# Attention and MLP decode: narrow matrix-vector products widened to 28 copies, the folded MLP weight rows loaded at the start, one scalar step moved

## The chip, the cores and the metric

The kernel runs on one core of one Trainium2 chip. The metric is the device time of one execution in microseconds (us), as the median of several runs; lower is better.

## The reference

One decode step for 8 requests. An attention block and an MLP block alternate, and both are applied twice with the same weights and the same caches:

```python
x = x + A(layernorm(x));  x = x + B(layernorm(x))     # layer 0
x = x + A(layernorm(x));  x = x + B(layernorm(x))     # layer 1
# A: q = x @ wq (448 -> 16 heads of 256); scores against k_cache (8 heads, 4096 keys, 256 wide,
#    two query heads on each), softmax, times v_cache, @ wo (4096 -> 448)
# B: hs = shifted(gelu(layernorm(x) @ w1)) @ w2;  x1 = x + hs
#    x1 + gelu(layernorm(x1) @ w3) @ w4              (448 -> 1792 -> 448)
```

With one token per request the shifts bring in zeros alone, so the kernel computes no w1 and no w2. One request's K cache is 16 MB in bf16, its V cache as much. Each layer needs all of both, for all 8 requests.

## The kernel before, in words

**Tiles and slots.** The unit of loading is a quarter of one head's K or V: 128 partitions of 2048 bf16 values, 512 KB. On-chip memory has 30 slots of that size (`QUARTERS`). The queue of SyncE (SP) loads the units in a fixed order into free slots (`load`, `issue_kv`, line 645); up to four units of one head become one load if neighbouring slots are free at that moment (`next_kv`). Some K and V units of a request (`KEEP_K`, `KEEP_V`) stay in their slots from layer 0 to layer 1, so that they are read once. A slot is freed by the PE instruction that reads it last, and SP waits for that instruction before it loads the slot again.

**One head.** `front` transposes K on TensorE (PE, L1509), VectorE (DVE) and ScalarE (ACT) copy the result back into the slot (L1440, L1441), PE makes the scores (in rows, L1405, or in 48 columns, L1148), and DVE, GpSimd (POOL) and ACT make the softmax. `back` multiplies by V (PV, L1275: eight matmuls with 256 columns per unit, four of them side by side in the array), adds the four partial rows (L1311) and multiplies by wo (L1339).

**Requests.** For each request b the kernel does layer 0 of some heads, then `mid(b)`, which is the layer 0 MLP and the layer 1 queries, and then layer 1, mixed with layer 0 of the next request. While `mid(b)` runs, the V units of the next request's heads arrive one by one as loads of 512 KB, each into a slot that a PV has just freed.

**The narrow products.** In `mid` a single vector of 448 or 1792 values meets a weight matrix. The weights are the stationary operand (128x128 blocks), the vector is the moving operand, one column wide. The kernel lets the same column stream several times (`bcast`, a step of zero), which gives as many equal result columns. Three families use it: the queries (`q_mms`, L901, `QW` copies, from `second_queries` and `column_sums`), the first MLP product (`h_mms`, L917, `HW` copies, called H here) and the second MLP product (`y_mm` in `mlp`, L1065, `YW` copies, called Y). Q and H step by one column from block to block: the copies of a block are overwritten by the next block, and only the first column of each stays. Y steps by `YW` columns, so its five blocks lie side by side. The last MLP, for two requests together, uses `HW // 2` columns (`dst is None`), the one for six requests uses none.

**Folded rows.** 448 = 3 x 128 + 64. The last 64 rows of w3 lie folded in `w3x_sb`: columns 0 to 895 on partitions 0 to 63, columns 896 to 1791 on partitions 64 to 127. wq's last rows lie in `wqx_sb` in the same way; there one half is loaded by SP and the other by ACT's queue, both at the start (`load_wq`). w3x is loaded by SP, both halves, with w3 (`load_rest`, due place 18).

**The order of the work.** `Plan` records every operation with a priority and a duration in microseconds, and `schedule` writes down the order of each engine in advance. `pe()` gives a narrow product n matmuls times `width` columns; the planner adds the columns of each piece of 3.413 us and takes the full-clock duration if the piece before had at least 3000 (`COLS`). Where PE is idle for over 0.1 us it puts in fillers (L1716, identity matmuls without use for the result) unless the last 3.413 us already hold 3500 columns (`TARGET`). The slots, and so how many units one load takes, follow from the planned times.

**The end.** After the last head, `last_stats`, `mlp(dst=None)`, `last_scale(1)` and `last_rows` make the last two requests' output: tanh on ACT (L1037), hT on DVE (L1046), four scalars `lin` on DVE (L828, L830, L836) that scale the residual row `xs` (L965), 56 matmuls (L973) and the sum `o_last` (L979).

Of the kernel before, what the change touches and what calls it, by code (L numbers as in the profile page):

```python
# [6 lines left out]
P = 128  # L7
B = 8
D = 448
# [3 lines left out]
NC5 = 5  # L13
# [32 lines left out]
LAST_AT = (-3, -2, -1)  # L46
PV0 = 0
PV1 = 0
QW, HW, YW = 24, 24, 12
SC = 448  # L50
YC = 0
ST = 504
# [423 lines left out]
def bass_interleave_layers__gqa_block_cached__mixer_s_mlp__decode_kernel(  # L476
# [20 lines left out]
    plan = Plan()  # L497
# [6 lines left out]
    def sb(name, shape, dt):  # L504
        n = 4 if dt in (f32, i32) else 2
        for s in shape[1:]:
            n *= s
        al = 32 if n >= 128 else 8
        cursor[0] = (cursor[0] + al - 1) // al * al
        t = nc.alloc_sbuf_tensor_at(name, shape, dt, offset=cursor[0], align_bytes=al)  # L510
        cursor[0] += (n + al - 1) // al * al
        assert cursor[0] <= high0, (name, cursor[0], high0)
        return t
# [5 lines left out]
    w3x_sb = sb("w3x_sb", [P, F // 2], bf)  # L519
    w4_sb = sb("w4_sb", [P, 14 * D], bf)  # L520
# [30 lines left out]
    lin = sb("lin", [P, 2, 2], f32)  # L551
# [5 lines left out]
    hT = sb("hT", [P, NB], bf)  # L557
# [54 lines left out]
    def bcast(ap, shape, axis):  # L612

        dims = [list(x) for x in ap.ap]
        dims.insert(axis, [0, shape])
        return bass.AP(tensor=ap.tensor, offset=ap.offset, ap=dims)
# [8 lines left out]
    def dma(name, dst, src, nbytes, sem, val, wr, at, row=8192):  # L625

        us = nbytes / 16 / 26.88e3 + nbytes / row / 16 * 0.008
        plan.op("sp", lambda eng: eng.dma_start(dst, src), us / FASTER, name, wr=wr, prio=at,  # L628
                dma=(sem, val))

    def dma_once(name, parts, keys, at, also=()):

        for i, (dst, src, nbytes, *row) in enumerate(parts):
            dma(name, dst, src, nbytes, nc.alloc_semaphore(f"s_{name}{i}"), 16,
                [keys[i], *(also if i == 0 else ())], 4 * at - 0.5, *row)
# [49 lines left out]
    def const_c(v):  # L685
# [7 lines left out]
            wr=["sel"])  # L693
# [7 lines left out]
    for bank, key in [(psR, "R"), (psM, M)]:  # L701
        plan.op("dve", lambda v, bank=bank: v.memset(bank[:, :], 0.0), 0.5, "const",
                wr=["psM", ("row", 0), ("row", 1)], banks=[key])
# [7 lines left out]
    def dv(fn, dur=0.13, rd=(), wr=(), banks=(), name="chain", prio=None):  # L711
        if prio is None:
            prio = urge[0] + len(plan.ops)
        return plan.op("dve", fn, dur, name, rd=rd, wr=wr, banks=banks, prio=prio)
# [6 lines left out]
    def pe(fn, n, rd=(), wr=(), banks=(), name="chain", prio=None, width=20):  # L721

        if prio is None:
            prio = urge[0] + len(plan.ops)
        d = 0.06 + 0.026 * n
        return plan.op("pe", fn, (d, max(d, 0.06 + n * width / 1200), width * n, n), name, rd=rd, wr=wr, banks=banks, prio=prio)
# [59 lines left out]
    def factor(k, c, v, rd, dv=dv):  # L786


        x, t, y = (z[:, k, c:c + 1] for z in (var, rst, rsy))
        a, b = (KK * (1.0 + LN_EPS) / D, KK * LN_EPS * LN_EPS) if k else (KK / D, KK * LN_EPS)  # L790
        dv(lambda e: e.tensor_scalar(x, v, a, b, ALU.mult, ALU.add), rd=rd, wr=[("x", k, c)])
        newton(x, t, y, ("t", k, c), [("x", k, c)], ("y", k, c), dv)
# [26 lines left out]
    def last_scale(r):  # L819


        c = B - 2 + r
        y, sf = rsy[:, 0, c:c + 1], self_f[:, r:r + 1]
        mm = mom[:, 2, 4 * r + 1:4 * r + 2]
        if r == 0:
            factor(0, c, mom[:, 2, 4 * r:4 * r + 1], [("v", r)])
        add = self_f[:, 0:1] if r == 0 else lin[:, 0, 0:1]
        dv(lambda v: v.tensor_scalar(lin[:, r, 0:1], y, sf, add, ALU.mult, ALU.add),  # L828
           rd=[("y", 0, c), "sel_f"] + [("lin", 0, 0), "hT"] * r, wr=[("lin", r, 0)])
        dv(lambda v: v.tensor_scalar(lin[:, r, 1:2], y, sf, mm, ALU.mult, ALU.mult),  # L830
           rd=[("y", 0, c), ("mm", r), "sel_f"], wr=[("lin", r, 1)])
        if r == 0:
            dv(lambda v: v.tensor_tensor(lin[:, 0, 0:1], lin[:, 0, 0:1], self_f[:, 1:2], ALU.add),
               rd=[("lin", 0, 0), "sel_f"], wr=[("lin", 0, 0)])
        else:
            dv(lambda v: v.tensor_tensor(lin[:, 1, 1:2], lin[:, 1, 1:2], lin[:, 0, 1:2], ALU.add),  # L836
               rd=[("lin", 0, 1), ("lin", 1, 1)], wr=[("lin", 1, 1)])
# [148 lines left out]
    def mlp(src, skey, n, dst, dkeys, rows_open=False):  # L986

        few = n < 3
        ch, kb, bk = where[0]
        at = SC if few else 0  # L990
        yw, yc = (YW, SC) if few else (n, 0)
        m = 14 * n
        h_, a_, hT_ = (hb[:, 0:m], g1[:, 0:m], hT) if few else (hb6[:, 0:m], g16[:, 0:m], hT6)
        GK, HK = (["g1", "xc", "yb"], ["hT"]) if few else (KH, KH)
# [4 lines left out]
        if dst is None:  # L999
# [3 lines left out]
               rd=[*skey] + W3, wr=[kb], banks=[bk], width=HW)  # L1003
            for r in range(n):
                scaled(r, rsy[:, 1, B - 2 + r:B - 1 + r], [("y", 1, B - 2 + r)])
        elif few:

            c = B - 2
# [7 lines left out]
            for mts in H_PARTS:  # L1016
                pe(lambda t, mts=mts: h_mms(t, lambda kc: src[:, kc, 0:n], ch, at, n, HW, mts), 4 * len(mts),
                   rd=[skey] + W3, wr=[kb], banks=[bk], width=HW)
# [5 lines left out]
        else:  # L1024
            norm(src, skey, True, n)
            pe(lambda t: h_mms(t, lambda kc: yb6[:, kc, 0:n], ch, 0, n, n), 56,
               rd=KH + W3, wr=[kb], banks=[bk])
# [4 lines left out]
           rd=HB, wr=GK)  # L1032
        dv(lambda v: v.scalar_tensor_tensor(a_, a_, GELU_K, h_, ALU.add, ALU.mult),
           rd=HB + GK[:1], wr=GK[:1] + ["a2"])
        if dst is None:
            minus_mean(mom[:, 2, 5:6], psR[:, ST + 2:ST + 3], [("ss", 1), "a2"], ("mm", 1), ["R"])
        plan.op("act", lambda a: a.activation(a_, a_, ACT.Tanh), 0.3, "chain",  # L1037
                rd=GK[:1], wr=GK[:1], prio=urge[0] + len(plan.ops))
        if few and dst is not None:
# [3 lines left out]
               rd=["mm", "mask", skey], wr=["base"])  # L1043
            dv(lambda v: v.scalar_tensor_tensor(bs, bs, rsy[:, 0, B - 2:B - 1], src[:, :, 0], ALU.mult, ALU.add),
               rd=["base", ("y", 0, B - 2), skey], wr=["base"])
        dv(lambda v: v.scalar_tensor_tensor(hT_[:, 0:m], a_, 1.0, h_, ALU.add, ALU.mult),  # L1046
           rd=HB + GK[:1], wr=HK)
# [5 lines left out]
        def y_mm(t, mts):  # L1053
            last = None
            for mt in mts:
                for fc in range(14):
                    r = hT_[:, fc * n:(fc + 1) * n]
                    if not few:
                        last = dup(t, ch, yc + mt * yw, yw, w4_sb, fc * D, mt, r, fc == 0, fc == 13)
                        continue  # L1060
                    a = fc * D + (mt * P if mt < 4 else D - P)
                    if mt == 3 and fc == 13:
                        last = dup(t, ch, yc + mt * yw, yw, w4_sb, fc * D, mt, bcast(r, yw, 1), False, True)
                        continue
                    last = t.matmul(ch[:, yc + mt * yw:yc + (mt + 1) * yw], w4_sb[:, a:a + P], bcast(r, yw, 1),  # L1065
                                    start=(fc == 0), stop=(fc == 13), skip_group_check=(mt == 3))
            return last
        parts = Y_PARTS if few else [range(NC5)]
        for mts in parts:
            pe(lambda t, mts=mts: y_mm(t, mts), 14 * len(mts), rd=HK + W4, wr=[kb], banks=[bk], width=yw)  # L1070
        ps4 = ch[:, yc:yc + NC5 * yw].rearrange("p (a n) -> p a n", n=yw)[:, :, 0:n]
        if few:
            yh = ymk[:, :].rearrange("p (a n) -> p a n", n=1)
            dv(lambda v: v.scalar_tensor_tensor(yh, ps4, 0.5, mask[:, :].rearrange("p (a n) -> p a n", n=1), ALU.mult,
# [4 lines left out]
           rd=[kb, "base"], wr=dkeys, banks=[bk])  # L1079

    def dup(t, dst, at, n, w, a, mt, rhs, start, stop):

        if mt < 3:
            return t.matmul(dst[:, at:at + n], w[:, a + mt * P:a + (mt + 1) * P], rhs, start=start,
                            stop=stop)
        g = 64 * (mt - 3)
        return t.matmul(dst[g:g + 64, at:at + n], w[:, a + 3 * P:a + D], rhs, start=start,
                        stop=stop, skip_group_check=True, tile_position=(0, g))  # L1090
# [479 lines left out]
    def load_wq():  # L1570
        dma_once("wq", [(wq_sb[:, kc, :], A_wq[kc * P:(kc + 1) * P, :], 1 << 20)
                        for kc in range(3)], ["wq0", "wq1", "wq2"], 2)
        dma_once("wqx", [(wqx_sb[0:64, :], A_wq[384:D, 0:2048], 1 << 19)], ["wqx0"], 0.05)
        s_wqx = nc.alloc_semaphore("s_wqx1")
        plan.op("act", lambda a: a.dma_start(wqx_sb[64:P, :], A_wq[384:D, 2048:4096]), 0.1, "wqx1",
                wr=["wqx1"], prio=0, dma=(s_wqx, 16))

    def load_rest():
        dma_once("wo", [(wo_sb[:, :].rearrange("p (t n) -> p t n", n=2 * D),
                         A_wo.rearrange("(t m c) n -> m t (c n)", m=P, c=2), 3670016, 1792)], ["wo0"], 6)  # L1580
        dma_once("w3", [(w3_sb[:, kc, :], B_w3[kc * P:(kc + 1) * P, :], 458752)
                        for kc in range(3)], ["w30", "w31", "w32"], 18)
        dma_once("w3x", [(w3x_sb[0:64, :], B_w3[384:D, 0:896], 114688 * 2),
                         (w3x_sb[64:P, :], B_w3[384:D, 896:1792], 114688 * 2)], ["w3x0", "w3x1"], 18)
    def load_w4():
        w4s = B_w4.rearrange("(s f) n -> s f n", s=2)
        dma_once("w4", [(w4_sb[:, 7 * i * D:(7 * i + 6) * D].rearrange("p (t n) -> p t n", n=2 * D),
                         w4s[i, 0:768].rearrange("(t m c) n -> m t (c n)", m=P, c=2), 688128, 1792)
                        for i in range(2)] +
                 [(w4_sb[:, (7 * i + 6) * D:(7 * i + 7) * D], w4s[i, 768:896], 114688, 896)  # L1590
                  for i in range(2)], ["w40", "w41", "w42", "w43"], 20, ["xr0", "xr1", "xr2"])
# [75 lines left out]

    load_wq()
    load_rest()
    first_queries()  # L1670
    load_w4()
# [104 lines left out]
```

## Time and profile before

| | |
|---|---|
| Time, median of 3 runs (lowest, highest) | 1078.7 us (1078.3, 1079.33) |
| The profiled execution's own time | 1076.9 us |
| its span, first to last instruction | 1075.1 us |
| Mean granted TensorE clock | 0.935 |
| Read from device memory | 434.18 MB, 404 GB/s over the span |
| PE, DVE, ACT busy | 943.7, 588.3, 343.7 us |

The profile is one execution taken by the hardware profiler. Its page gives busy times, the span in 40 slices (busy shares in tenths, PEclk the granted clock in tenths, DMA the share of its 16 engines, GB/s), the load queues, the chain of work that ended last, and groups of equal instructions. The trace behind it can be asked by stretch: a row "A:B" then gives the stretch in us from the span's start, its length, the busy us of each engine with its instructions in brackets, the granted clock, the share of the DMA engines and GB/s; a row for one line of the code has only the engines that it uses. In rows in order of time the columns are start, length, engine, line, operation, output and inputs, shape, and count; "PE" is the matmul itself, "PEld" its weight load, "SPq" the queue of SP. Matmuls overlap: one of 24 columns lasts 183 ns from its start to its end, but the next starts long before that.

### The profile page before, as it was taken

The numbers are of one execution on the slowest core, as the hardware profiler recorded it, in microseconds if no ns is written. First come the engines' busy times: TensorE is split into PE (matmuls) and PEld (weight loads), VectorE is DVE, ScalarE is ACT, GpSimd is POOL, SyncE is SP. The second block draws the span as 40 slices with busy tenths as digits, with TensorE's granted clock in tenths as the row PEclk, the third lists the DMA queues.
The fourth block names the chain that finished last, engine by engine and source line by source line (L and its number), as shares of the span: only waits on it lengthen the run. The fifth ranks groups of instructions, "written<-read, shape, count | busy, mean of one in ns | idle before, by whom it ended". The sixth has DMA issues, their size and how long they took to land.

```text
span 1075.1 us, 34110 instructions
## 1 busy us (share of the span) xinstructions
PE 943.7 (88%) x15206; PEld 649.6 (60%) x15206; DVE 588.3 (55%) x1879; ACT 343.7 (32%) x946; POOL 99.6 (9%) x284
## 2 busy tenths in 40 slices
PE   4989798898989989898989889998898899998996
PEld 4556555565656656566566655666555676666574
DVE  4345455555555556555565555555555656566474
ACT  1235113341234403254133431334223441343140
POOL 0000010010100101011010100100011000111011
PEclk9799899998999989999899998999999988999696
DMA  9999999999999999999999999999999999999995
GB/s 353 408 425 424 390 407 424 424 422 402 406 424 426 417 400 420 425 426 403 387 424 426 424 413 399 425 425 424 396 408 424 426 393 394 397 423 416 329 426 232
DMA packets 56526, 436.39 MB, mean 406 GB/s; under 512 B 6062, under 2 KB 9276, under 8 KB 34236
## 3 DMA queue, kind: packets, MB, share of 16 engines
q1 hardware_dynamic: 56292, 433.95, 98.4%
q8 instruction: 119, 1.95, 0.7%
q10 hardware_dynamic: 88, 0.26, 0.1%
q14 instruction: 27, 0.22, 0.1%
HBM read 434.18 MB, written 0.01 MB: 404 GB/s over the span
## 4 chain that ended last, share of the span: by engine, by line
DMA 56%; PE 36%; DVE 3%; SPq 2%; issue 1%; ACT 1%; POOL 0%; DVEq 0%
DMA kv<-in_A_k_cache_dram 32%; DMA kv<-in_A_v_cache_dram 23%; PE psT L1509 12%; PE psP L1275 7%; PE psT L1405 5%; PE psM L1148 3%; PE psR L1339 2%; SPq L628 2%; PE psM L1065 1%; PE psM L901 1%; DVE kv L1440 1%; DMA w_sb<-in_B_w_dram 1%; PE psP L1716 1%; PE psM L917 1%; SPq L645 1%
## 5 line engine op out<-in xcount | busy, mean ns | idle before, releaser
L1509 PE MATMUL psT<-ident_f,kv 128*128 128x128 f32 x2752 | 373.8, 283 | 37.1 <-DMA kv<-in_A_k_cache_dram 35.6
L1509 PEld LDWEIGHTS psT<-ident_f,kv 128*128 128x128 f32 x2752 | 301.6, 143 | 117.6 <-issue 54.9
L1440 DVE COPY kv<-psT 128x512 f32<-128x512 f32 x368 | 253.1, 691 | 196.8 <-PE psT L1509 189.2
L1441 ACT COPY kv<-psT 128x512 f32<-128x512 f32 x352 | 205.0, 586 | 386.9 <-PE psT L1509 301.9
L1275 PE MATMUL psP<-kv,pT 128*2 128x256 bf16 x4032 | 175.6, 290 | 18.8 <-DMA kv<-in_A_v_cache_dram 16.3
L1405 PE MATMUL psT<-kv,qz 128*32 128x512 bf16 x1664 | 133.7, 396 | 3.0 <-ACT kv L1441 1.9
L1275 PEld LDWEIGHTS psP<-kv,pT 128*2 128x2 bf16 x4032 | 81.7, 83 | 63.4 <-DMA kv<-in_A_v_cache_dram 25.6
L1228 POOL PARTITION_ALL_REDUCE gm<-pm x128 | 45.5, 355 | 772.7 <-DVE pm L1226 762.9
L1238 ACT ACTIVATE pT<-sS,nb,fac 128x32 bf16<-128x32 bf16 x128 | 52.6, 417 | 116.7 <-DVE nb L1232 116.7
L1301 DVE CAST oS<-psP 128x256 bf16<-128x256 f32 x126 | 53.3, 423 | 52.6 <-PE psP L1275 51.1
L1339 PE MATMUL psR<-wo_sb,oT 128*1 128x448 bf16 x444 | 62.6, 366 | 7.7 <-DVE oT L1318 4.0
L1242 POOL PARTITION_ALL_REDUCE Db<-rs x128 | 51.0, 398 | 182.9 <-ACT pT L1238 182.9
L1311 PEld LDWEIGHTS psP<-sel,oS 128*128 128x128 bf16 x504 | 23.0, 98 | 60.5 <-DVE oS L1303 54.4
L1311 PE MATMUL psP<-sel,oS 128*128 128x2 bf16 x504 | 31.8, 166 | 31.4 <-DVE oS L1303 29.4
L1238 ACT ACTIVATE pT<-sS,nb 128x32 bf16<-128x32 bf16 x128 | 40.8, 326 | 54.9 <-DVE nb L1232 54.9
L1716 PE MATMUL psP<-ident_f 128*128 128x256 bf16 x359 | 57.8, 288 | 0.0
L1405 PEld LDWEIGHTS psT<-kv,qz 128*32 128x32 bf16 x1664 | 34.5, 95 | 36.6 <-issue 13.3
L1420 DVE CAST sr<-psT 128x512 bf16<-128x512 f32 x55 | 38.0, 692 | 31.7 <-PE psT L1405 31.5
L1303 DVE TENSOR_TENSOR oS<-psP,oS 128x256 bf16<-128x256 f32 x126 | 53.3, 423 | 2.9
L1148 PEld LDWEIGHTS psM<-qz,kv 128*128 128x128 bf16 x1344 | 42.5, 100 | 17.2 <-issue 7.5
L1148 PE MATMUL psM<-qz,kv 128*128 128x48 bf16 x1344 | 49.5, 189 | 3.2 <-issue 1.3
L1421 ACT CAST sr<-psT 128x512 bf16<-128x512 f32 x49 | 28.7, 585 | 54.0 <-PE psT L1405 51.0
(197 smaller groups left out, 786.8 us busy)
## 6 DMA issues: line engine op xcount, KB each, us to landing
kv<-in_A_k_cache_dram SPq DMA_DIRECT2D x68, 2048.0 KB, 23.3
kv<-in_A_v_cache_dram SPq DMA_DIRECT2D x61, 2048.0 KB, 17.4
kv<-in_A_v_cache_dram SPq DMA_DIRECT2D x163, 512.0 KB, 8.3
kv<-in_A_k_cache_dram SPq DMA_DIRECT2D x12, 1536.0 KB, 17.7
kv<-in_A_k_cache_dram SPq DMA_DIRECT2D x28, 512.0 KB, 9.1
kv<-in_A_v_cache_dram SPq DMA_DIRECT2D x14, 1024.0 KB, 8.8
kv<-in_A_v_cache_dram SPq DMA_DIRECT2D x7, 1536.0 KB, 11.1
kv<-in_A_k_cache_dram SPq DMA_DIRECT2D x8, 1024.0 KB, 9.5
```

The costliest lines, as they stand in the source:

```text
L1148: last = t.matmul(ps[:, SB + 2 * i:SB + 2 * i + 2 * REP], a()[:, c:256:2], bcast(rhs(c), REP, 1), start=(c == 0), stop=(c == 1))
L1238: return a.activation(pT[nr][:, :, :].rearrange("p i j -> p j i")[:, jj, :], sview[:, jj, :], ACT.Exp, bias=nb[nm][:, jj:jj + 1], scale=sc ...
L1275: last = t.matmul(ps[g4:g4 + 2, PV0:PV0 + DH], pT[nr][:, k, :], slot_ap(q, s * 256, 256), start=(i < 4), stop=(i >= 28), skip_group_check= ...
L1301: plan.op("dve", lambda v: v.tensor_copy(oS[:, 0, :], po), 0.36, "o", rd=[("pv", par, x) for x in range(4)], wr=["oS0"], banks=[bk], prio=hi)
L1303: plan.op("dve", lambda v: v.tensor_tensor(oS[:, 1, :], po, oS[:, 0, :], ALU.subtract), 0.36, "o", rd=["oS0"] + [("pv", par, x) for x in r ...
L1311: last = t.matmul(ps[:, PV1 + 2 * c:PV1 + 2 * c + 2], oS[:, w, c:DH:2], sel[:, :], start=(w == 0), stop=(w == 1))
L1339: last = t.matmul(psR[r:r + 1, 0:D], oT[no][:, i % 2, i // 2:i // 2 + 1], wo_sb[:, a:a + D], start=(k == 1 and i < 2), stop=(k == turn_at ...
L1405: last = t.matmul(psT[bank][32 * g:32 * g + 32, :], qz[:, a:a + 32], slot_ap(qs[g // 2], g % 2 * 1024, 1024)[:, c:1024:2], start=(half == ...
L1440: return e.tensor_copy(dst, psT[bank][:, :])
L1441: return e.copy(dst, psT[bank][:, :])
L1509: last = t.transpose(psT[bank][:, s * P:(s + 1) * P], src, ident_f[:, :])
L1716: return t.matmul(dst, ident_b, bcast(ident_b[:, 0:n // 4], 4, 1), start=True, stop=True)
```

## The change

Three edits. (1) `QW` and `HW` go from 24 to 28. Y streams 28 copies (`YN`) instead of 12 and steps by one column, so that its blocks overlap as Q's and H's do; `YW` = 12 stays for the products with wo and for the row turn. (2) w3x leaves `load_rest`: SP issues its first half right behind wqx's, at the start, and ACT's queue the second half, behind wqx's second half. Its size is stated to the planner without the factor of two. (3) `last_scale(1)`'s second scalar step (L830) gets a dependence on hT, which the first step (L828) had already, so it stands behind hT on DVE.

```diff
-QW, HW, YW = 24, 24, 12
+QW, HW, YW = 28, 28, 12
+YN = 28
@@ last_scale
         dv(lambda v: v.tensor_scalar(lin[:, r, 1:2], y, sf, mm, ALU.mult, ALU.mult),
-           rd=[("y", 0, c), ("mm", r), "sel_f"], wr=[("lin", r, 1)])
+           rd=[("y", 0, c), ("mm", r), "sel_f"] + ["hT"] * r, wr=[("lin", r, 1)])
@@ mlp
-        yw, yc = (YW, SC) if few else (n, 0)
+        yw, yc, ys = (YN, SC, 1) if few else (n, 0, n)
@@ y_mm
-                    last = t.matmul(ch[:, yc + mt * yw:yc + (mt + 1) * yw], w4_sb[:, a:a + P], bcast(r, yw, 1),
+                    last = t.matmul(ch[:, yc + mt * ys:yc + mt * ys + yw], w4_sb[:, a:a + P], bcast(r, yw, 1),
                                     start=(fc == 0), stop=(fc == 13), skip_group_check=(mt == 3))
...
-        ps4 = ch[:, yc:yc + NC5 * yw].rearrange("p (a n) -> p a n", n=yw)[:, :, 0:n]
+        ps4 = ch[:, yc:yc + NC5 * ys].rearrange("p (a n) -> p a n", n=ys)
@@ load_wq
+        dma_once("w3x", [(w3x_sb[0:64, :], B_w3[384:D, 0:896], 114688)], ["w3x0"], 0.06)
+        s_w3x = nc.alloc_semaphore("s_w3x1")
+        plan.op("act", lambda a: a.dma_start(w3x_sb[64:P, :], B_w3[384:D, 896:1792]), 0.1, "w3x1",
+                wr=["w3x1"], prio=1, dma=(s_w3x, 16))
@@ load_rest
-        dma_once("w3x", [(w3x_sb[0:64, :], B_w3[384:D, 0:896], 114688 * 2),
-                         (w3x_sb[64:P, :], B_w3[384:D, 896:1792], 114688 * 2)], ["w3x0", "w3x1"], 18)
```

More of the change, by code (lines that the diff above doesn't have):

```diff
@@ L1058, in y_mm @@
                     if not few:
-                        last = dup(t, ch, yc + mt * yw, yw, w4_sb, fc * D, mt, r, fc == 0, fc == 13)
+                        last = dup(t, ch, yc + mt * ys, yw, w4_sb, fc * D, mt, r, fc == 0, fc == 13)
                         continue
@@ L1062, in y_mm @@
                     if mt == 3 and fc == 13:
-                        last = dup(t, ch, yc + mt * yw, yw, w4_sb, fc * D, mt, bcast(r, yw, 1), False, True)
+                        last = dup(t, ch, yc + mt * ys, yw, w4_sb, fc * D, mt, bcast(r, yw, 1), False, True)
                         continue
-                    last = t.matmul(ch[:, yc + mt * yw:yc + (mt + 1) * yw], w4_sb[:, a:a + P], bcast(r, yw, 1),
+                    last = t.matmul(ch[:, yc + mt * ys:yc + mt * ys + yw], w4_sb[:, a:a + P], bcast(r, yw, 1),
                                     start=(fc == 0), stop=(fc == 13), skip_group_check=(mt == 3))
```

## The prediction, made before the changed kernel ran

> **What bounds the kernel now.** I read the page's head, slices and queues first, then the table of stretches, then the order in time around one MLP.
>
> ```profile
> span 1075.1 us, 34110 instructions
> ...
> DMA  9999999999999999999999999999999999999995
> GB/s 353 408 425 424 390 407 424 424 422 402 406 424 426 417 400 420 425 426 403 387 424 426 424 413 399 425 425 424 396 408 424 426 393 394 397 423 416 329 426 232
> ...
> q1 hardware_dynamic: 56292, 433.95, 98.4%
> ```
>
> SP's one load queue takes 98.4% of 16 engines' span. The bytes are the same afterwards, so only three things can move the time: how fast bytes flow while the queue is full (424 to 426 GB/s in the good slices), how often it runs dry, and the two ends. The weak slices (390, 402, 400, 387 and so on) come once per request, where one request's MLP and the next request's 512 KB V loads meet. The next view is the table of stretches: an undisturbed plateau, a stretch in which 512 KB loads flow undisturbed, and the seven stretches between requests in which the granted clock falls.
>
> ```profile
> core 0: us, PE busy (x) PEld busy (x) DVE busy (x) ACT busy (x) POOL busy (x), PEclk, DMA share, GB/s
> 560.00:640.00 80.00, 71.70 (x917) 50.19 (x916) 44.28 (x115) 32.97 (x85) 7.53 (x20) 0.98 1.01 423
> 250.00:260.00 10.00, 7.73 (x158) 4.11 (x151) 4.97 (x17) 0.72 (x4) 0.75 (x2) 0.95 1.01 408
> ...
> 255.60:272.65 17.05, 16.05 (x343) 9.28 (x336) 8.47 (x48) 0.21 (x1) 0.00 (x0) 0.60 1.01 391
> 385.30:398.95 13.65, 12.88 (x285) 7.62 (x285) 7.59 (x46) 0.21 (x1) 0.00 (x0) 0.63 1.02 398
> 511.60:528.66 17.06, 15.21 (x347) 9.71 (x346) 8.80 (x49) 0.21 (x1) 0.00 (x0) 0.70 0.99 370
> 648.10:658.40 10.30, 9.18 (x204) 5.64 (x202) 4.62 (x26) 0.21 (x1) 0.00 (x0) 0.67 1.01 391
> 771.00:784.66 13.66, 13.05 (x300) 8.04 (x292) 7.48 (x46) 0.21 (x1) 0.00 (x0) 0.75 0.99 373
> 900.70:917.78 17.08, 16.36 (x366) 10.82 (x358) 8.31 (x48) 0.21 (x1) 0.00 (x0) 0.60 1.01 379
> 992.90:1013.36 20.46, 18.15 (x368) 11.37 (x365) 9.23 (x50) 0.22 (x1) 0.00 (x0) 0.58 0.91 323
> ```
>
> Small loads alone cost 423 to 408 GB/s. What a stretch has below 408 is time in which a load was issued late, because the PE had not yet freed its slot: 17.05 x (1 - 391/408) = 0.7, then 0.3, 1.6, 0.4, 1.2, 1.2 and 4.3, **9.7 us together**. That is all that a faster PE can win here. A mean clock of 0.60 means half speed in 0.8 of the stretch; so the seven hold 78 us at half speed, 23 pieces of 3.41 us.
>
> **Part 1, 28 copies.** First, what sets the clock. The rows of all engines for two adjacent pieces come first, then those of L917 and of L1275 in the first piece and of L901 in the second, then rows in order of time.
>
> ```profile
> 774.42:777.84 3.42, 3.42 (x75) 1.64 (x72) 2.96 (x21) 0.21 (x1) 0.00 (x0) 0.50 1.01 396
> 777.84:781.25 3.41, 3.41 (x108) 2.89 (x107) 0.72 (x4) 0.00 (x0) 0.00 (x0) 1.00 0.97 357
> 781.25:784.66 3.41, 3.41 (x62) 1.66 (x58) 2.29 (x14) 0.00 (x0) 0.00 (x0) 0.50 1.02 395
> ```
>
> ```profile
> 774.42:777.84 3.42, 1.34 (x44) 1.13 (x40) 0.50 1.01 396
> ```
>
> ```profile
> 774.42:777.84 3.42, 1.78 (x24) 0.31 (x24) 0.50 1.01 396
> ```
>
> ```profile
> 777.84:781.25 3.41, 0.35 (x14) 0.37 (x15) 1.00 0.97 357
> ```
>
> ```profile
> 776.06 0.59 PE L1716 MATMUL psP<-ident_f 128*128 128x256 bf16 x2
> 776.58 1.18 PE L1275 MATMUL psP<-kv,pT 128*2 128x256 bf16 x16
> 777.69 0.91 PE L1065 MATMUL psM<-hT,w_sb 128*128 128x12 bf16 x28
> 778.53 0.39 PE L1275 MATMUL psP<-kv,pT 128*2 128x256 bf16 x8
> 778.86 0.88 PE L1065 MATMUL psM<-hT,w_sb 128*128 128x12 bf16 x27
> ...
> 779.79 0.53 PE L1065 MATMUL psM<-hT,w_sb 128*128 128x12 bf16 x14
> 780.25 0.39 PE L1275 MATMUL psP<-kv,pT 128*2 128x256 bf16 x8
> ...
> 783.23 0.80 PE L1148 MATMUL psM<-qz,kv 128*128 128x48 bf16 x16
> 783.96 0.60 PE L1275 MATMUL psP<-kv,pT 128*2 128x256 bf16 x8
> 784.49 0.62 PE L1148 MATMUL psM<-qz,kv 128*128 128x48 bf16 x16
> ...
> 785.45 0.72 PE L1148 MATMUL psM<-qz,kv 128*128 128x48 bf16 x22
> ```
>
> PE is busy throughout both pieces, yet after the first the clock rises and after the second it falls. The difference is columns streamed. First piece: L917 44 x 24 = 1056, PV 24 x 256 / 4 = 1536 (four PV matmuls share the array), two fillers 512, about 3,100. Second: the Y product 70 x 12 = 840, PV 16 x 64 = 1024, the query's 14 x 24 = 336: 2,200. With 28 copies the second holds 1960 + 1024 + 392 = 3,380, above the first. So I expect the fall at 781 not to come. Every stretch has such a Y piece (+1120 columns) and an H piece (56 x 4 = +224).
>
> What wider products cost: at full clock 22 matmuls of 48 columns take 0.72 us, less one latency of 0.18 some 26 ns each, so 28 columns can't cost more than that; the 12-column rows give (0.88 - 0.17) / 26 = 27 ns. At half clock 24 columns take 1.34/44 = 30 ns and 48 take (783.96 - 783.23) / 16 = 46 ns; 28 lies between 30 and, on a straight line, 33. Nearest row 24: I take 0. At 33, 142 widened matmuls of a stretch would add 0.4 us of PE time.
>
> What full clock gives: a group of eight PV takes 0.53 us at half clock (783.96 to the next row at 784.49) and 0.33 us at full (778.53 to 778.86), so a piece with three groups frees its slots 0.6 us earlier. Load time is won only where the queue is dry. Without the last stretch, in which PE itself waits (18.15 busy of 20.46), six stretches lose 5.4 us in 18 half-speed pieces, 0.30 us each. I expect ten of these to run at full clock: **-3.0 us**. Ends: 0, if other waits end last, and -6, with the last stretch's share.
>
> The page *TensorE: Matmul & The Clock Gate* of the Trainium skill, section "Why this matters for your kernels", has another rule: some 4 us of continuous work brings full clock. By that rule copies bring nothing and the sum lacks this term; the trace disagrees, since PE was busy 3.41 of 3.41 us before the clock fell.
>
> **Part 1's side effect.** The planner counts columns, so it writes another order. In the two programs' instruction orders the cache loads are now 372 instead of 361: 203 of 512 KB for 191, 29 of 1 MB for 22, 13 of 1.5 MB for 19, 127 of 2 MB for 129. 512 KB (0.524 MB) takes 1.285 us at 408 GB/s and 1.240 at 423, 0.045 to 0.06 us per extra cut, eleven cuts: **+0.6 us**. Ends 0 and +1.1 (all 19 more small loads).
>
> **Part 2, the folded w3 rows.**
>
> ```profile
> 1.52 0.57 SPq L628 DMA_DIRECT2D wqx_sb<-in_A_wq_dram  x1
> 2.13 1.46 SPq L645 DMA_DIRECT2D kv<-in_A_k_cache_dram  x2
> ...
> 106.97 1.11 SPq L628 DMA_DIRECT2D w3x_sb<-in_B_w_dram  x2
> ```
>
> ```profile
> 2.00:7.00 5.00, 1.39 (x41) 1.25 (x41) 1.89 (x16) 0.62 (x1) 0.29 (x1) 1.00 0.90 233
> ```
>
> ```profile
> PE psM L917 <- DMA w3x_sb<-in_B_w_dram: 1.9, 1, 1.9
> ```
>
> At 107 us two loads of 112 KB leave SP's queue: 0.23 MB at 423 GB/s is 0.54 us of load time won. At the start one such load is issued on SP ahead of the first K load, by the wqx row 0.57 us, so that all loads behind it come 0.57 later while the engines have room (233 GB/s); ACT's half uses ACT's queue, ahead of its table load, with nothing behind it that is due. **0 us**, ends -0.5 and +0.6. The 1.9 us that PE waits for w3x at 118 us goes, but the same PE run then waits for w3 itself, issued just ahead, and for w4, and the queue is full there: nothing.
>
> **Part 3, the last scalars.**
>
> ```profile
> 1070.52 0.27 DVE L830 TENSOR_SCALAR lin<-rsy,self_f,mom 128x1 f32<-128x1 f32 x1
> 1070.71 0.18 DVE L1046 SCALAR_TENSOR_TENSOR hT<-g,hb 128x28 bf16<-128x28 f32 x1
> ```
>
> ```profile
> 1070.26 0.23 ACT L1037 ACTIVATE g<-g 128x28 f32<-128x28 f32 x1 [16.16 <-DVE g L1033]
> ```
>
> The tanh ends at 1070.49; hT starts at 1070.71 behind L830. With L830 moved behind hT, hT starts some 0.17 us earlier, and the last 56 matmuls with it; L830 then lies beside them. **-0.2 us**, ends 0 and -0.2. No DMA has work left there, so it counts in full.
>
> **Sum.** -3.0 + 0.6 + 0 - 0.2 = -2.6 us. The profiled execution took 1076.9 us (span 1075.1 and 1.8 around it), 1.8 below the median of 1078.7; by its own time 1074.3, on the median **1076.1 us**. The own range of this case is 1073 to 1078.
>
> **Rivals.**
> 1. *The clock rises and the loads don't notice.* The slots are freed in time anyway, or the next wait (DVE's moments between Y and the queries, SP's issue) ends last. For it: in the piece from 777.84 the clock was 1.00 and only 357 GB/s flowed, and the DMA share is 0.99 or more in all stretches but the last. Against it: the weak GB/s and the low clocks coincide. Time: 1078.7 + 0.6 - 0.2 = 1079.1.
> 2. *Slower: longer runs of fillers in front of PV.* The new order holds 441 fillers for 432; in the third request's stretch (385 us) eight stand in one run between queries and scores (one before), and there and in the stretch before it nine instead of seven ahead of the row turn. Two fillers take 0.52 us at half clock (776.06 to 776.58), so eight hold PV, and with it SP's next load, 2.1 us. It decides as soon as less than that is left in the queue, at 1.29 us per 512 KB load. The last stretch shows what a dry queue costs: 4.3 us. Two such runs: +4.2 + 0.4, **1083.3**. Against it: fillers stand where the planner sees PE idle.
> 3. *All stalls go.* -9.7 + 0.4 = 1069.4. Against it: the last stretch's stalls have PE idle.
> 4. *Busy time, not columns, decides the clock.* Then no piece changes its clock and the first term is 0: 1079.1 as in rival 1. For it: PE is idle for 1 us or more in four of the seven stretches (17.05 less 16.05 in the first). Against it: PE was busy 3.41 of 3.41 us in the piece before the fall at 781.25. This is the rule that the page cited above from the Trainium skill gives.
> That the widening doesn't happen is no case: the changed program's matmuls have 28 columns.
>
> **How the numbers follow.** Forecast 0.49, rival 1 0.21, rival 2 0.18, rival 3 0.07, rival 4 0.05. A measurement of this kernel can tell about 0.2%, 2.2 us, from no change. Of the forecast's own spread some seven in ten lie below 1076.5, the rest within 0.2%: faster 0.35 + 0.07 = 0.42, same 0.14 + 0.21 + 0.05 = 0.40, slower 0.18. Range 1072.5 to 1081.0: it takes in rivals 1 and 4 and the ends of the unknown costs, and leaves out rival 3 and two thirds of rival 2, under 0.2.
>
> **What would show it.** Right: mean granted clock from 0.935 to about 0.95, no fall after a Y piece, the stretches between requests at 395 GB/s or more, L1065's mean time little changed, hT right behind the tanh. Wrong: the clock up and the stretches' GB/s as before (rival 1); a stretch under 370 GB/s with a run of L1716 ahead of PV (rival 2); the first K data later by more than 0.6 us.

## The result, and the profile after

The changed kernel took 1073.45 us (median of 7 runs, 1071.74 to 1077.13), the kernel before 1078.3 us (7 runs, 1075.95 to 1079.33) on the same chip: a ratio of **0.9962**, interval 0.995 to 0.9973, some 4.1 us; the two medians by themselves differ by 4.9 us. A second series gave 0.9964 (0.9952 to 0.9977). One execution differs from the next by 1 to 3 us, so below, ratios come from series and single profiles only serve to see where something happens. The forecast of 1076.1 was 2.6 us too high, and the range held.

The page of the changed kernel, first the rows that answer to those of before:

```profile
span 1069.8 us, 34153 instructions
...
PEclk9899999999999989999999999999999998999896
...
GB/s 364 409 425 424 408 391 426 424 422 404 406 427 424 420 396 419 426 426 418 385 424 424 422 403 386 426 425 425 397 402 425 427 419 387 407 425 416 381 422 229
...
q1 hardware_dynamic: 57796, 433.84, 98.6%
```

It is still bound by SP's load queue, and the good slices still flow at 424 to 427 GB/s. The weak ones are still there (391, 396, 385, 386, 387); what differs most is the last weak slice, 381 where it was 329.

The table of stretches, at the same seven places between requests (each moved by as much as its MLP moved; columns as in the prediction: length, busy us of the engines, granted clock, DMA share, GB/s):

```profile
256.18:273.23 17.05, 14.35 (x376) 9.67 (x365) 8.95 (x51) 0.77 (x3) 0.00 (x0) 1.00 1.01 386
385.62:399.27 13.65, 12.70 (x311) 8.80 (x315) 7.16 (x43) 0.21 (x1) 0.00 (x0) 0.77 1.00 381
509.66:526.71 17.05, 14.53 (x380) 9.84 (x377) 9.11 (x49) 0.21 (x1) 0.00 (x0) 0.90 0.99 376
647.05:657.35 10.30, 9.15 (x242) 6.05 (x241) 5.36 (x28) 0.21 (x1) 0.00 (x0) 1.00 0.99 360
770.65:784.31 13.66, 12.26 (x324) 8.44 (x324) 7.63 (x46) 0.21 (x1) 0.00 (x0) 1.00 1.02 387
897.93:915.01 17.08, 15.91 (x358) 10.08 (x355) 8.54 (x48) 0.30 (x2) 0.00 (x0) 0.60 0.98 375
989.48:1009.94 20.46, 17.69 (x415) 12.11 (x415) 8.98 (x52) 0.49 (x2) 0.00 (x0) 0.83 1.01 389
```

This is the surprise. The clock did what was predicted: in the first six stretches it is 0.60 to 1.00 where it was 0.60 to 0.75, and of their 18 half-speed pieces seven are left (ten had been expected to run at full clock, eleven do; the sixth stretch stays at 0.60). PE is busy for 78.9 us of these six where it was for 82.7. But the loads did not follow: 386, 381, 376, 360, 387, 375 GB/s for 391, 398, 370, 391, 373, 379. By the prediction's own formula (length x (1 - GB/s / 408)) these six lose 0.9 + 0.9 + 1.3 + 1.2 + 0.7 + 1.4 = 6.4 us; before it was 5.4. The seventh loses 1.0 us where it lost 4.3. So the time did not come from where the clock term had put it.

The piece with the second MLP product (Y), with the 3.41 us behind it; first the order in time, then the stretches:

```profile
777.14 1.32 PE L1066 MATMUL psM<-hT,w_sb 128*128 128x28 bf16 x42
```

```profile
777.14:780.55 3.41, 3.41 (x96) 2.68 (x93) 0.34 (x2) 0.00 (x0) 0.00 (x0) 1.00 1.01 405
780.55:783.96 3.41, 3.10 (x86) 2.03 (x87) 2.70 (x15) 0.00 (x0) 0.00 (x0) 1.00 1.02 399
```

The fall behind Y is gone here, with 28 columns in each of its matmuls (the 42 take (1.32 - 0.18) / 41 = 28 ns each; 12 columns took 27).

The end, in order of time: the tanh, hT, the last matmuls' weight loads, and the scalar step that was moved.

```profile
1065.14 0.23 ACT L1038 ACTIVATE g<-g 128x28 f32<-128x28 f32 x1 [15.24 <-DVE g L1034]
1065.40 0.19 DVE L1047 SCALAR_TENSOR_TENSOR hT<-g,hb 128x28 bf16<-128x28 f32 x1
...
1065.89 0.27 DVE L831 TENSOR_SCALAR lin<-rsy,self_f,mom 128x1 f32<-128x1 f32 x1
```

hT starts 0.03 us behind the tanh (0.22 before), and from the tanh's start to the end of the span it is 4.66 us where it was 4.84. That part is as predicted.

### The profile page after: what moved, and what is told of

Same layout as the page of the kernel before. It is cut to its first block, busy times and chain, and to the rows that moved or that the text cites. A ratio compares the mean times of both kernels' runs of the same rounds, so it can differ in the third digit from the quotient of the medians.

```text
span 1069.8 us, 34153 instructions
## 1 busy us (share of the span) xinstructions
PE 937.8 (88%) x15215; PEld 650.7 (61%) x15215; DVE 586.8 (55%) x1879; ACT 345.6 (32%) x946; POOL 99.6 (9%) x284
## 4 chain that ended last, share of the span: by engine, by line
DMA 56%; PE 36%; DVE 4%; issue 2%; SPq 1%; ACT 1%; POOL 0%
DMA kv<-in_A_k_cache_dram 30%; DMA kv<-in_A_v_cache_dram 26%; PE psT L1510 11%; PE psP L1276 8%; PE psT L1406 5%; PE psM L1149 3%; PE psM L902 2%; PE psR L1340 2%; PE psP L1719 1%; SPq L629 1%; PE psM L918 1%; DMA w_sb<-in_B_w_dram 1%; DVE oS L1304 1%; DVE oS L1302 1%; PE psP L1312 1%
## 5 line engine op out<-in xcount | busy, mean ns | idle before, releaser
L1441 DVE COPY kv<-psT 128x512 f32<-128x512 f32 x364 | 250.4, 691 | 186.4 <-PE psT L1510 179.2
L1442 ACT COPY kv<-psT 128x512 f32<-128x512 f32 x356 | 207.9, 586 | 376.3 <-PE psT L1510 300.3
L1276 PE MATMUL psP<-kv,pT 128*2 128x256 bf16 x4032 | 170.9, 281 | 26.3 <-DMA kv<-in_A_v_cache_dram 24.3
L1222 DVE CAST sS<-psM 128x64 bf16<-128x64 f32 x128 | 28.1, 219 | 41.3 <-PE psM L1149 28.4
```

Source lines behind the costliest of these rows:

```text
L1276: last = t.matmul(ps[g4:g4 + 2, PV0:PV0 + DH], pT[nr][:, k, :], slot_ap(q, s * 256, 256), start=(i < 4), stop=(i >= 28), skip_group_check= ...
L1441: return e.tensor_copy(dst, psT[bank][:, :])
L1442: return e.copy(dst, psT[bank][:, :])
```

## The experiments

The labels carry the number of the experiment (e4 is experiment 4). The theory was that of the prediction, with w3x's start added after the result: the copies raise the clock, PV comes earlier, the queue is dry less often. The rival: only the order that the planner wrote moved the time.

The change mixes three things: the copies that the chip streams, the place of w3x, and the order that the planner writes because it counts other columns (with it goes the moved scalar step). They can be separated. The planner can be told one number and the chip given another; then the order stays and only the widths differ. And after the planner is done, w3x's two loads can be moved by hand in the queues, all else staying. So each of the eight combinations is a kernel: order old or new, copies old or new, w3x late or early.

| order | copies | w3x | ratio to before, interval | clock, mean of the runs |
|---|---|---|---|---|
| old | old | late (kernel before) | 1 | 0.934 |
| old | 28 | late (e2_wide) | 0.9994, 0.9981 to 1.0007 | 0.950 |
| old | old | early (e8_b_early) | 0.9990, 0.9976 to 1.0004 | 0.937 |
| old | 28 | early (e10_wide_early) | 0.9991, 0.9981 to 1.0002 | 0.952 |
| new | old | late (e9_order) | 0.9981, 0.9970 to 0.9993 | 0.937 |
| new | 28 | late (e6_late) | 0.9979, 0.9962 to 0.9995 | 0.952 |
| new | old | early (e1_narrow) | 0.9985, 0.9969 to 1.0001 | 0.937 |
| new | 28 | early (changed kernel, e5_again) | 0.9962 and 0.9964 | 0.953 |

A least-squares fit of three separate effects to the 190 single times of these kernels and of the kernel before (one level for each series, residual spread 1.75 us) gives **order -1.6 +- 0.6 us, early w3x -0.85 +- 0.6, copies -0.6 +- 0.6**. Any of the three effects' joint terms is smaller than its uncertainty (that of all three -1.9 +- 2.7), so whether the copies are worth more in the new order is open.

**The copies alone, in either order.** Edits, in the new and in the old order:

```diff
+EQ, EH, EY = 24, 24, 12     # e1_narrow: planner still told 28; e2_wide: 28, 28, 28, planner told 24, 24, 12
-  ... q_mms(..., SC, 1, QW), 32, ..., width=QW)
+  ... q_mms(..., SC, 1, EQ), 32, ..., width=QW)      # H and Y likewise
```

> The changed kernel's instruction order on all engines and its w3x loads, but the chip streams the old 24, 24 and 12 copies; only the planner still counts 28. Theory A (the columns on the chip raise the clock, PV comes earlier, the load queue is dry less often): the mean granted clock falls to about 0.935 to 0.94 and the time goes back to 1076 to 1079 us (ratio 0.998 to 1.001 to the kernel before). Rival B (only the planner's rewritten order moved the time): 1073.5 us, ratio 0.996, as the changed kernel, whatever the clock does.

> The old kernel's instruction order and its w3x loads, but the chip streams 28 copies in all three products (Y stepping by one column); the planner still counts 24, 24 and 12. Theory A (columns on the chip): clock about 0.95, no fall behind the second MLP products, 1075 to 1076 us, ratio 0.997 to 0.998. Rival B (order alone): 1078.3 us, ratio 1.000, whatever the clock does.

e1_narrow: 0.9985 at clock 0.937; e2_wide: 0.9994 at clock 0.950. The clock follows the copies in both, whatever the order. The first time lies at the low end of theory A's range (0.998 to 1.001) and not at rival B's 0.996; the second is rival B's 1.000 within its interval and not theory A's 0.997 to 0.998. So neither theory has both: taking the copies out of the changed kernel costs 0.0022, by the single times 2.2 +- 1.4 us, and putting them into the kernel before wins next to nothing. The page and the clock view of e2_wide, which has the instruction order of the kernel before:

```profile
PE 942.3 (88%) x15206; PEld 656.3 (61%) x15206; DVE 588.1 (55%) x1879; ACT 343.8 (32%) x946; POOL 99.6 (9%) x284
```

```profile
core 0: 1074.1 us, clock 0.947
```

PE is as busy as before (943.7 us then) and the clock is 0.947 for 0.935: columns streamed move it, not busy time. That ends rival 4. The time of this kernel, at a higher clock and in the same order, is that of the kernel before within the interval.

**40 copies.** `EQ, EH, EY = 40, 40, 40` in the new order.

> The changed kernel's order with 40 copies on the chip instead of 28. Theory A: clock 0.955 to 0.965 and 1072 to 1074 us, unless the matmuls now take longer than their weights: by the 48-column rows of before 0.040 us each at half clock, so about 33 ns here for 27, which over some 224 matmuls of a request's narrow products is at most 1.3 us where the clock is at half, and then 1074 to 1076. Rival B: 1073.5 us, as the changed kernel.

Measured 1.000 (0.9986 to 1.0013) at a mean clock of 0.965, the highest of all: some 4 us slower than with 28 copies. Both theories missed. The first 55 Y matmuls of the last `mid` in e3_forty, in e7_26 (26 copies) and in the kernel before (12), in order of time, and 32 score matmuls of the changed kernel, whose 48 columns are a pair of neighbouring columns repeated 24 times (`REP` in the kernel); 40 and 48 at full clock, 26 and 12 at half:

```profile
1007.60 2.24 PE L1067 MATMUL psM<-hT,w_sb 128*128 128x40 bf16 x55
```

```profile
1002.96 1.65 PE L1067 MATMUL psM<-hT,w_sb 128*128 128x26 bf16 x55
```

```profile
1001.79 1.61 PE L1065 MATMUL psM<-hT,w_sb 128*128 128x12 bf16 x55
```

```profile
1013.47 0.96 PE L1149 MATMUL psM<-qz,kv 128*128 128x48 bf16 x32
```

Less one latency of 0.18 to 0.22 us, 40 copies take 38 ns a matmul, 26 and 12 take 27, and the 48 columns of the repeated pair only 25. So copies of one single column go through at about 1 ns each, and they are free just up to 27 or 28. A request has 56 + 70 + 128 such matmuls; 10 ns more on each is 2.5 us of PE time per request, and the page of e3_forty has PE busy for 951.8 us where the changed kernel has 937.8. That this is what the 40 lost, on a faster clock, is the likely reading; no run tested it by itself.

**26 copies.** `EQ, EH, EY = 26, 26, 26`, the last MLP's 14 kept.

> The changed kernel's order and w3x, 26 copies streamed instead of 28 (the last MLP keeps its 14). In the traces a repeated column streams at about 1 ns whatever the granted clock (28 copies: 28 ns between the second MLP's matmuls, 40 copies: 38 ns, 12 copies: 27 ns), so 26 would hide behind the 27 ns of a weight load. If that is what 40 copies lost, 26 copies keep the clock of 28 (about 0.953) and win 0.1 to 0.2 us in each of the seven stretches at most: 0 to 1.5 us faster than the changed kernel, ratio 0.995 to 0.996. Rival (the piece's columns fall under the gate's bound again): clock 0.945 or less and slower than the changed kernel.

0.9963 (0.994 to 0.9986), clock 0.950: neither number, the same as 28 copies as far as this can be measured. It is no better version.

**w3x, undone with a new plan and by hand.** e4_now3x takes the second edit of the change back in the source, so that the planner writes a third order; e6_late and e8_b_early move the loads in an order that stays:

```diff
     plan.schedule()
+    a, b = ...          # e6_late: w3x's halves, out of SP's and ACT's start,
+    sp[i:i] = [a, b]    # and behind w3 on SP; e8_b_early: the other way round
```

> The changed kernel without its second edit: w3x is loaded with w3 by the SP queue alone, both halves. If the early w3x fills load engines that are idle at the start, the first 5 MB land some 0.7 us later against the clock of the changed kernel, another 1.2 us goes where w3 and w4 load (107 to 120 us), and the time is 1074.5 to 1075.5 us, ratio 0.997 to 0.998. Rival (the start's gain is given back before the end, as the prediction's 0 for this edit has it): 1073.5 us, ratio 0.996.

> The changed kernel with every engine's order kept, except that both halves of w3x are moved by hand, after the planner is done, to SP's queue behind w3, where the kernel before has them; 28 copies stay. Theory A (the early w3x itself is worth time, because its 128 packets of 1792 bytes run at 300 to 350 GB/s in the full queue from 114.5 to 118.5 us): 1.0 to 1.5 us slower than the changed kernel, ratio 0.997 to 0.998. Rival B (the loss of experiment 4 came from the order that the planner wrote for it, not from w3x): as the changed kernel, 0.996. If the loss is as large as in experiment 4 (3.5 to 4 us, ratio 1.000), w3x carries the change alone.

> The kernel before with every engine's order kept, except that w3x's two halves are moved by hand to the start, one on SP behind wqx's first half, one on ACT's queue behind wqx's second half; 24, 24 and 12 copies stay. Theory A (the early w3x itself is worth time): 1.0 to 1.5 us faster than the kernel before, ratio 0.9985 to 0.999, clock unchanged at 0.934. Rival B (it is worth nothing, or the gain at 107 to 120 us is given back at the next full slot): ratio 1.000.

e4_now3x: 0.9998 (0.9986 to 1.0011), e6_late: 0.9979, e8_b_early: 0.999. The two hand-moved ones agree with the theory (1.6 us against the changed kernel of the same series, 1.1 us against the kernel before), but their intervals (0.9962 to 0.9995 and 0.9976 to 1.0004) take in the rival's numbers too; the rows below show the gain at its place. The first kept neither its theory's number nor its rival's: it differs from e6_late by 2 us, at the edge of the noise, although the chip has the same edits in both; only the order differs. The loads at w3x's old place, five us of the kernel before, of e8_b_early, of the changed kernel and of e6_late:

```profile
114.00:119.00 5.00, 3.26 (x55) 1.61 (x51) 2.50 (x9) 0.72 (x4) 0.75 (x2) 1.00 1.09 336
```

```profile
114.00:119.00 5.00, 4.19 (x89) 2.51 (x86) 2.50 (x9) 0.72 (x4) 0.75 (x2) 1.00 1.07 443
```

```profile
114.00:119.00 5.00, 2.30 (x39) 1.10 (x40) 2.37 (x9) 0.72 (x4) 0.75 (x2) 0.99 1.06 441
```

```profile
114.00:119.00 5.00, 2.33 (x41) 0.99 (x37) 2.51 (x9) 0.72 (x4) 0.75 (x2) 1.00 1.09 333
```

336 and 333 GB/s with w3x there, 443 and 441 without: 5 x (1 - 335/442) = 1.2 us, in either order. By the ends of the packets in the traces, the nine profiles with the early w3x take 25.4 to 25.6 us from 37 to 47.7 MB landed, the five with the late one 26.4 to 26.9.

**Order and copies at their last corners.** e9_order is e1_narrow with w3x moved back, so that the order alone is left; e10_wide_early is e2_wide with w3x moved forward, so that all is there but the order.

> The changed kernel's order with the old 24, 24 and 12 copies and with w3x moved back behind w3 by hand: what is left of the change is the order that the planner wrote for 28 columns, and the scalar step. From the other corners: experiment 1 (0.9985) less the 0.0010 to 0.0016 that the early w3x was worth in experiments 8 and 6 gives 0.9995 to 1.000. Theory A (w3x and the copies carry the change): 0.999 to 1.001. Rival B (the order carries it): 0.998 or less.

> The kernel before in its own order with 28 copies and with w3x moved to the start by hand: both edits without the planner's new order. If the edits add up (0.9994 from experiment 2, 0.9990 from experiment 8): 0.9983 to 0.9985. If the copies bring 2 us only where the order is written for them (experiment 1 against the changed kernel), it stays there, 0.0020 above the changed kernel; if the order brings nothing of its own, 0.9965.

e9_order: 0.9981, between the two theories and nearer to rival B; e10_wide_early: 0.9991, above all three numbers, with the sum of the edits inside its interval. So the order has the largest share by these numbers, though by the fit it is not clear of w3x's: alone it gives half of the gain, and both other edits without it give a quarter, which is not told apart from nothing. Where it acts is seen in the 25 us from the first MLP product of the last `mid`. The stretches view of the kernel before, of e2_wide, of e9_order and of the changed kernel:

```profile
997.82:1022.82 25.00, 23.12 (x530) 15.07 (x528) 12.12 (x54) 3.11 (x11) 1.51 (x4) 0.69 0.93 322
```

```profile
998.67:1023.67 25.00, 23.66 (x552) 16.41 (x548) 14.08 (x63) 3.69 (x12) 1.51 (x4) 0.87 0.95 350
```

```profile
997.64:1022.64 25.00, 23.82 (x545) 16.77 (x544) 14.15 (x69) 4.23 (x13) 1.50 (x4) 0.80 1.00 379
```

```profile
994.40:1019.40 25.00, 22.28 (x532) 15.78 (x533) 13.52 (x67) 3.36 (x12) 1.50 (x4) 0.86 1.00 375
```

With the old order the DMA share is 0.93 and 0.95, with the new one 1.00, and the clock does not sort them: 0.87 goes with 350 GB/s, 0.80 with 379. The other five profiles of the eight kernels agree: 328 and 325 GB/s at a share of 0.93 and 0.91 in the old order (e8_b_early, e10_wide_early), 378, 388 and 383 at 1.00 to 1.02 in the new one (e6_late, e1_narrow, e5_again). It does not hold for every execution: e12_w4early below, which has the new order but for two loads, shows 337 GB/s at 0.95, in an execution of 1078.9 us where its median is 1073.85. What PE does behind the Y products, in order of time in the kernel before and in e9_order, both with 12 copies in Y:

```profile
1003.49 0.54 PE L1065 MATMUL psM<-hT,w_sb 128*128 128x12 bf16 x14
1003.96 0.91 PE L1339 MATMUL psR<-wo_sb,oT 128*1 128x448 bf16 x4
1004.80 0.27 PE L772 MATMUL psM<-x2c 128*128 128x3 bf16 x4
1005.00 0.60 PE L1275 MATMUL psP<-kv,pT 128*2 128x256 bf16 x8
```

```profile
1001.77 0.54 PE L1341 MATMUL psR<-wo_sb,oT 128*1 128x448 bf16 x4
...
1003.93 0.53 PE L1067 MATMUL psM<-hT,w_sb 128*128 128x12 bf16 x14
1004.39 1.02 PE L1277 MATMUL psP<-kv,pT 128*2 128x256 bf16 x16
1005.35 0.27 PE L774 MATMUL psM<-x2c 128*128 128x3 bf16 x4
```

In the new order the product with wo stands ahead of Y, and 16 PV matmuls, which free two slots, come right behind Y. In the old one wo and the sums come first, and then 8 PV. It is one of several moves in that stretch; which of them keeps the queue full was not tried.

**Other orders with the same edits.** e11_told30 tells the planner 30 and streams 28.

> The changed kernel with 28 copies on the chip and the planner told 30, which gives another order of all engines (order of 2384 PE rows for 2374), the edits on the chip being the same. If orders written by this planner differ by chance as in experiment 4 against experiment 6 (0.9998 and 0.9979 with the same edits), this lands anywhere from 0.996 to 0.999; if the edits alone decide, 0.9963 to 0.9965 as the changed kernel.

0.9997 (0.9983 to 1.0011), clock 0.951. Both edits are on the chip, the clock is up, and nothing is won. It is clear of the changed kernel's 0.9962 and 0.9964, and above the range that was expected. With e4_now3x, which has w3x late, it is the second of three new orders with which nothing is won: the gain of the changed kernel's order is not something that every order written for wider products brings. By these three it looks like a lucky draw.

**w4's short rows at the start too.** In the new order, w4's last two loads are moved by hand from SP to ACT's queue behind w3x.

> A version that may beat both: the changed kernel in its order, with the two 112 KB loads of w4's last rows (128 rows of 896 bytes each) moved by hand from SP's queue behind w4 to ACT's queue at the start, behind w3x's second half. If short rows in the full queue are what the late w3x cost (its 229 KB cost 1.25 us at their place in every kernel that has them there), the same bytes in half as long rows cost 1.0 to 1.5 us there, and at the start they cost the first 5 MB 0.5 to 1 us: 0 to 1 us faster than the changed kernel, ratio 0.9953 to 0.9965. Rival (the start has no room left, its engines being busy from 2.5 us on): 0 to 1 us slower, 0.9965 to 0.9975.

0.997 (0.9957 to 0.9982), 1073.85 us: not better than the changed kernel (0.9962, 0.9964), nor told apart from it. In its profile 5 MB have landed 0.4 to 0.7 us later than in the other kernels with the new order and early w3x, which points to the rival. No kernel here beats the changed one.

## Why the number held and its reasons did not

- **What bounds the kernel.** Right: the queue before and after, and the seven stretches as the places to look at.
- **The clock.** The step "what sets the clock" was right: 0.935 became 0.954, the fall behind Y went where it was shown, and e2_wide shows that the copies alone do it. The Trainium skill, page *TensorE: Matmul & The Clock Gate*, section "Why this matters for your kernels", asks for some 4 us of continuous work; e2_wide disagrees with busy time as the rule, at 942.3 us of PE for 943.7.
- **What full clock gives, -3.0 us.** This step failed. It shared out the 5.4 us that six stretches lost among their half-speed pieces, 0.30 us each, as if the half speed had caused the loss. Weak flow and low clock lie together, but copies without a new order gave 0.9994 and, with w3x early in both, 0.9991 for 0.9990; over all pairs -0.6 +- 0.6 us. In the changed kernel's profile the six stretches lose 1.0 us more than before, not less. The same shows in all nine profiles of the eight kernels: in the 27 us from the first MLP product of the second to the seventh `mid`, the old copies have a mean clock of 0.80 to 0.82 and 392 GB/s, 28 copies 0.87 to 0.93 and 390 GB/s (means of four and five profiles). One pair of the four says otherwise in time, the one next to the changed kernel (e1_narrow, 2.2 +- 1.4 us); whether the copies are worth that much once order and w3x are in place stays open. What the six stretches show is rival 1's mechanism: the clock rises and the loads don't notice. A likely reason for the coincidence, argued only: when PE waits for V data it streams fewer columns, and the clock falls after it.
- **The last stretch.** The prediction set it aside because PE waits there. It held the largest gain, 3.3 us in the two profiles, and it came with the order (e9_order, at clock 0.80, and the profiles named above). The fit gives the order less, 1.6 us; part of the gain there seems to be lost again elsewhere.
- **What wider products cost, 0.** Right within what counts: 27 became 28 ns, 28 to 29 at half clock. The upper end of 33 was too high: the 48-column row on its straight line is a repeated pair, which says little of a single column.
- **The side effect of the new order, +0.6.** Wrong in sign and in what was counted: -1.6 +- 0.6 us, of which some 0.2 is the scalar step by the rows above. Eleven more cuts of the loads were priced; that the list puts PV elsewhere was not, and can't be read from counts.
- **w3x, 0 with ends -0.5 and +0.6.** Wrong in size: 1.2 us at its place, -0.85 +- 0.6 in all. The step took its bytes at 423 GB/s; the trace has 336 GB/s while its 128 packets of 1792 bytes go through, and that loss of rate goes too. The later first K load came as the step has it (issued at 2.89 us for 2.13, by the row below and the prediction's), and cost nothing that can be seen: 5 MB had landed at 15.9 to 16.4 us in eight profiles with the early w3x (e12_w4early left out) and at 15.6 to 16.8 in five without.

The order in time on SP's queue in the changed kernel:

```profile
2.12 0.73 SPq L629 DMA_DIRECT2D w3x_sb<-in_B_w_dram  x1
2.89 1.24 SPq L646 DMA_DIRECT2D kv<-in_A_k_cache_dram  x2
```

- **The last scalars, -0.2.** Right: hT's wait of 0.22 us became 0.03.
- **Rival 2.** Longer filler runs were priced at 2.1 us each. The stretch named there, at 385 us, loses 0.9 for 0.3 us; nothing of the size forecast.
- **Rival 3.** Of the 9.7 us that the seven stretches lost by the prediction's formula 7.4 are left.

So the sum of -2.6 came near the measured -4.1 by luck, by two misses that cancel: a clock term of -3.0 that was worth about -0.6, and the order (with the scalar step) and w3x, worth -2.4 together where +0.4 had been written. The separate effects add up to -3.0; the last 1.1 us, if they are not chance, belong to the edits jointly, and that stays open.

## What to carry to other kernels

Where a list scheduler writes the order, an edit of a modelled cost is two edits: freeze the order and change only the chip's side, and the other way round, before crediting the time to the operation. Two things that are weak at the same moment (clock and flow here) are no price for one another; only a run that moves one of them alone gives it. And price a small load in a full queue by the flow while its packets go through, not by its bytes.

## What the runs showed of the hardware

- Copies of one single column (read with a step of zero) go through TensorE at about 1 ns a copy: 28 ns for 28, 38 ns for 40, at full clock, where 48 columns that repeat a pair 24 times take 25. Overlapping result columns alone don't cost this, since the scores' overlap as well. Whether it is the reading of one address, or that Y adds into the same columns 14 times in a row and the scores twice, was not separated.
- The granted clock follows the streamed columns at the same busy time (0.934 to 0.950 by copies alone), and 0.965 with 40 copies in the new order; in the profiles the flow of the loads did not rise with it.
- 128 packets of 1792 bytes among larger ones brought the flow from 442 down to 335 GB/s over 5 us.
- Orders written by the same planner for the same edits differ by 2 us, at the edge of the noise (late w3x: 0.9979 and 0.9998), and by 3.6 us, clear of it (early w3x: 0.9962 and 0.9964 against 0.9997): nearly as much as the change is worth.
